# Packing the remainder rows and pacing the attention work of a four-layer transformer kernel

## The chip, the cores and the metric

The kernel runs on one core of one Trainium2 chip. The metric is the device time of one execution in microseconds (us). The engines are named as the profile names them: PE is TensorE (PEld its weight loads), DVE is VectorE, ACT is ScalarE, POOL is GpSimd. "L326" in a profile line is line 326 of the kernel's source. All runs quoted here were of the fast state. A ratio is the mean time of one kernel's fast runs over that of the other's of the same rounds, so not quite the ratio of the medians quoted beside it.

## The reference, cut to what matters

```
x = A_x                                               # 2048 tokens, 576 features
x = x + A(layernorm(x), A_wqkv, A_wo)
x = x + B(layernorm(x), B_w_gate, B_w_up, B_w_down)
x = x + A(layernorm(x), A_wqkv, A_wo)                 # the same weights again
x = x + B(layernorm(x), B_w_gate, B_w_up, B_w_down)

A: q, k, v = x @ wqkv, 32 heads of 18; a token attends to 8 tokens, itself and
   those 2, 4, .. 14 before it; softmax; @ wo
B: h = (x @ w_gate) * (x @ w_up)   # 576 -> 4608
   h @ w_down                      # 4608 -> 576
```

Both kernels work on chunks of 256 tokens. With 8 chunks and two layers of each kind there are 16 units of A (attention) and 16 stages of B (feed-forward). In B nearly all work is PE's. In A the products of q and k and the weighted sums of v are elementwise work on DVE, between short stretches of PE: transposes, projections, logits, broadcast of the weights, output. B of a chunk needs A of the same chunk and layer, and the second A of a chunk needs its first B.

## The kernel before

The parts that the argument touches. A bank is one of the buffers into which PE writes its sums (`psum` in the code); here ACT and DVE empty it before the next sum begins in it:

```
gu = [psum.tile([P, 2, CH], FP32, name=f"gu{i}") for i in range(2)]     # two gate/up banks
pa = [psum.tile([P, 512], FP32, name=f"pa{i}") for i in range(2)]       # two banks for A
...
def gate_up(ft):                      # one feature tile of 128, of 36
    ...
    ps = gu[ft % 2]
    for (hh, w_) in ((0, wg), (1, wu)):
        for k in range(KT):           # KT = 5: four full tiles and the remainder of 64 rows
            nc.tensor.matmul(ps[:, hh, :], lhsT=w_[:, k, ft * P:(ft + 1) * P], rhs=xnT[:, k, :], ...)
    ...
        nc.scalar.copy(g_sb[:], ps[:, 0, :])
        nc.vector.tensor_tensor(hT[:], ps[:, 1, :], g_sb[:], op=ALU.mult)
...
gate_up(0)
for ft in range(1, NFT):
    gate_up(ft)
    down(ft - 1)                      # down is one feature tile behind
...
for k in range(max(nA - 1, nB)):      # the whole of A comes ahead of B in the program
    ia = k + 1
    if ia < nA:
        a_head(ia)
        _drain(a_body(ia))
    if k < nB:
        for _ in b_body(k): ...       # b_head(k + 1) at two thirds of it
```

The order in which an engine takes its instructions is fixed when the program is compiled. The compiler's scheduling starts from the order of the program but moves instructions (the first experiment below shows it: six remainders of gate that were written ahead of six of up came out partly in pairs with them). That each engine then runs its own list in order on the chip is taken for granted here and was not tested.

Of the kernel before, what the change touches and what calls it, by code (L numbers as in the profile page):

```python
# [14 lines left out]
def _drain(gen):  # L15
    for _ in gen:
        pass


@with_exitstack  # L20
def kernel(
# [10 lines left out]
    nlayers: int = 4,  # L32
    mode: str = "seq",
# [8 lines left out]
    KT = (D + P - 1) // P  # L42
    DP = KT * P
    DHP = KT * 4
    CH = 256
    NCH = S // CH
    NST = CH // P
    SQ = CH // 4
    NFT = F // P
    G = 4  # L50
    while NFT % G:
        G -= 1
    qscale = float(Dh) ** -0.5
    assert D == 576 and S % CH == 0 and F % P == 0
# [4 lines left out]
    xbp = ctx.enter_context(tc.tile_pool(name="xbp", bufs=4))  # L59
    psum = ctx.enter_context(tc.tile_pool(name="psum", bufs=1, space=PSUM))  # L60
    st_pool = ctx.enter_context(tc.tile_pool(name="static", bufs=1))
    small = ctx.enter_context(tc.tile_pool(name="small", bufs=6))

    xv = A_x.rearrange("b (n p) d -> (b n) p d", p=P)
    ov = out.rearrange("b (n p) d -> (b n) p d", p=P)

    NXS = 3
    xf = [[xpool.tile([P, D], FP32, name=f"xf{s}_{i}") for i in range(NST)] for s in range(NXS)]

    def load_x(c):  # L70
        for i in range(NST):
            xb = xbp.tile([P, D], BF16, name="xb")
            nc.sync.dma_start(xb[:], xv[c * NST + i])
            nc.scalar.copy(xf[c % NXS][i][:], xb[:])  # L74

    nc.scalar.preload_act_table_set("natural_log_exp_and_others")
    load_x(0)

# [3 lines left out]
                            base=0, pattern=[[-1, P]], channel_multiplier=1)  # L82
    eps_t = consts.tile([P, 1], FP32, name="eps_t")
    nc.vector.memset(eps_t[:], 1e-5)
    xn_bufs = [st_pool.tile([P, DP], BF16, name=f"xnb{i}") for i in range(2)]
    for t_ in xn_bufs:
        nc.gpsimd.memset(t_[:, D:DP], 0.0)

    wqkv = wpool.tile([P, KT, 3, DHP, 32], BF16, name="wqkv")
    wo_p = wpool.tile([P, KT, D], BF16, name="wo_p")  # L90
    wg = wpool.tile([P, KT, F], BF16, name="wg")
    wu = wpool.tile([P, KT, F], BF16, name="wu")
    ksz = [min(P, D - k * P) for k in range(KT)]
    TL = D - (KT - 1) * P

    def load_rows(dst, src):
        for k in range(KT):
            nc.sync.dma_start(dst[:ksz[k], k, :], src[k * P:k * P + ksz[k], :])
        nc.sync.dma_start(dst[TL:2 * TL, KT - 1, :], src[(KT - 1) * P:D, :])

    startup_pool = tc.tile_pool(name="startup", bufs=1)
    sp = startup_pool.__enter__()
    wraw = sp.tile([P, KT, 3 * D], BF16, name="wraw")
    load_rows(wraw, A_wqkv)
    if NCH > 1:
        load_x(1)
    wo_v = A_wo.rearrange("(h d) n -> d h n", d=Dh)
    for d in range(DHP):
        t, g = d // 4, d % 4
        dd = d if d < Dh else d - 2  # L110
        nc.sync.dma_start(wo_p[32 * g:32 * g + 32, t, :], wo_v[dd])
    if nlayers > 1:
        load_rows(wg, B_w_gate)
        load_rows(wu, B_w_up)
    wd_v = B_w_down.rearrange("(g t p) d -> g p t d", p=P, t=G)

    accm = [psum.tile([P, 512], FP32, name=f"accm{i}") for i in range(NST)]
    acct = psum.tile([P, NST, 64], FP32, name="acct")
    gu = [psum.tile([P, 2, CH], FP32, name=f"gu{i}") for i in range(2)]
    pa = [psum.tile([P, 512], FP32, name=f"pa{i}") for i in range(2)]  # L120
    tps = psum.tile([P, KT, P], BF16, name="tps")

    NXT = 4
    xnT_bufs = [st_pool.tile([P, KT, CH], BF16, name=f"xnT{i}") for i in range(NXT)]
    qT = st_pool.tile([P, KT, CH], BF16, name="qT")
    kT = st_pool.tile([P, KT, HALO + CH], BF16, name="kT")
    vT = st_pool.tile([P, KT, HALO + CH], BF16, name="vT")
    Lt = st_pool.tile([P, W, SQ], FP32, name="Lt")
    a_c = st_pool.tile([P, W, SQ], BF16, name="a_c")
    ab = st_pool.tile([P, W, 4, SQ], BF16, name="ab")  # L130
    oT = st_pool.tile([P, KT, CH], BF16, name="oT")

    Erep = consts.tile([P, 4, 32], BF16, name="Erep")
    Erep2 = Erep[:].rearrange("p a b -> p (a b)")
    Bsel = consts.tile([P, 4, 4, 32], BF16, name="Bsel")
    n_alayers = (nlayers + 1) // 2
    halo_k = [consts.tile([P, KT, HALO], BF16, name=f"halo_k{l}") for l in range(n_alayers)]
    halo_v = [consts.tile([P, KT, HALO], BF16, name=f"halo_v{l}") for l in range(n_alayers)]
    wqf = wqkv[:].rearrange("p k t d h -> p k t (d h)")
    rot_box = {}  # L140

    def finish_startup():
        nc.gpsimd.memset(wqkv[:, :, :, Dh:DHP, :], 0.0)
        for t_ in halo_k + halo_v:
            nc.gpsimd.memset(t_[:], 0.0)
        for k in range(KT):
            src = wraw[:, k, :].rearrange("p (t h d) -> p t d h", t=3, h=H)
            if k % 2 == 0:
                nc.vector.tensor_copy(wqkv[:, k, :, 0:Dh, :], src)
            else:  # L150
                nc.scalar.copy(wqkv[:, k, :, 0:Dh, :], src)
        startup_pool.__exit__(None, None, None)
        nc.gpsimd.memset(Erep[:], 0.0)
        for g0 in range(4):
            nc.gpsimd.affine_select(out=Erep[:], in_=Erep[:], compare_op=ALU.not_equal, fill=1.0,
                                    base=-32 * g0, pattern=[[0, 4], [-1, 32]], channel_multiplier=1)
        nc.gpsimd.memset(Bsel[:], 0.0)
        for j in range(4):
            nc.gpsimd.affine_select(out=Bsel[:, j], in_=Bsel[:, j], compare_op=ALU.not_equal, fill=1.0,
                                    base=-32 * j, pattern=[[0, 4], [-1, 32]], channel_multiplier=1)  # L160
        rot_box["rot"] = ctx.enter_context(tc.tile_pool(name="rot", bufs=2))

    state = {"xn": 0, "pa": 0}
    wlist = [w ^ 1 for w in range(W)]

    def head(c, xnT):
        for i in range(NST):
            x = xf[c % NXS][i]
            st = small.tile([P, 2, 6], FP32, name="st")
            xr = x[:].rearrange("p (a b) -> p a b", a=2)  # L170
            for a in range(2):
                nc.vector.bn_stats(out=st[:, a, :], in_=xr[:, a, :])  # L172
            mv = small.tile([P, 2], FP32, name="mv")
            nc.vector.bn_aggr(out=mv[:], in_=st[:])
            rstd = small.tile([P, 1], FP32, name="rstd")
            nc.scalar.activation(rstd[:], mv[:, 1:2], ACT.Ln, bias=eps_t[:])
            nc.scalar.activation(rstd[:], rstd[:], ACT.Exp, scale=-0.5)
            nmr = small.tile([P, 1], FP32, name="nmr")
            nc.vector.tensor_scalar(nmr[:], mv[:, 0:1], rstd[:], -1.0, op0=ALU.mult, op1=ALU.mult)  # L179
            xn = xn_bufs[state["xn"] % 2]  # L180
            state["xn"] += 1
            nc.scalar.activation(xn[:, 0:D], x[:], ACT.Identity, bias=nmr[:], scale=rstd[:])  # L182
            for k in range(KT):
                nc.tensor.transpose(tps[:, k, :], xn[:, k * P:(k + 1) * P], ident[:])  # L184
            nc.scalar.copy(xnT[:, :, i * P:(i + 1) * P], tps[:])  # L185
            yield

    def next_pa():
        b = state["pa"] % 2
        state["pa"] += 1  # L190
        return b

    def phase_A(c, la, xnT, last):
        xs = xf[c % NXS]
        nc.scalar.copy(kT[:, :, 0:HALO], halo_k[la][:])
        nc.scalar.copy(vT[:, :, 0:HALO], halo_v[la][:])
        for t3, dst in ((0, qT), (1, kT), (2, vT)):
            for t in range(KT):
                b = next_pa()
                for k in range(KT):  # L200
                    nc.tensor.matmul(pa[b][:, 0:CH], lhsT=wqf[:, k, t3, t * P:(t + 1) * P], rhs=xnT[:, k, :],  # L201
                                     start=(k == 0), stop=(k == KT - 1))
                if t3 == 0:
                    nc.scalar.mul(dst[:, t, :], pa[b][:, 0:CH], qscale)
                else:
                    nc.scalar.copy(dst[:, t, HALO:HALO + CH], pa[b][:, 0:CH])  # L206
                yield
        nc.scalar.copy(halo_k[la][:], kT[:, :, CH:CH + HALO])
        nc.scalar.copy(halo_v[la][:], vT[:, :, CH:CH + HALO])
        for p_ in range(W // 2):  # L210
            prod = rot_box["rot"].tile([P, 2, KT, CH], BF16, name="prod", bufs=2)
# [12 lines left out]
            for j in range(4):  # L224
                nc.scalar.copy(Lt[32 * j:32 * j + 32, 2 * p_:2 * p_ + 2, :], lgv[32 * j:32 * j + 32, :, SQ * j:SQ * (j + 1)])  # L225
# [149 lines left out]
    if nB:  # L375
        b_head(0)
# [41 lines left out]
```

## Time and profile before

| | before |
|---|---|
| median time | 1268.2 us (12 runs, 1266.9 to 1269.5) |
| profiled span | 1267.2 us |
| first gate matmul, end of the last matmul | 71.3, 1263.2 us |
| length of a B stage in the middle | 75.5 us |

A window of one middle stage of the kernel before. The columns are the stretch and its length, busy us and instructions of each engine, granted PE clock, DMA share and GB/s:

```profile
core 0: us, PE busy (x) PEld busy (x) DVE busy (x) ACT busy (x) POOL busy (x), PEclk, DMA share, GB/s
451.80:527.30 75.50, 73.34 (x619) 54.29 (x628) 46.10 (x100) 34.22 (x94) 0.00 (x0) 1.00 0.24 72
```

No engine but PE is near the length of the stage, and DMA is at a quarter. PE's 73.3 us are busy time of overlapping records. The matmuls of the stage (B's 56.9 us and one A unit of 13.5) take 70.4 us by their spacing, so about 5 us of the 75.5 are loss. Stages are counted here from the last down matmul of one stage to that of the next.

The profile's view of what PE waited for, kernel before (total us, times, longest):

```profile
PE tps L184 <- ACT xnb L182: 19.3, 4, 11.2
PE pa L253 <- DVE a_c L249: 15.2, 16, 6.7
PE pa L272 <- DVE oT L266: 12.3, 1, 12.3
PE pa L222 <- DVE s L220: 7.6, 15, 4.6
PE accm L312 <- DVE hT L305: 7.1, 24, 0.6
```

The large ones with few counts are the start-up. This view shows only waits that outlast the modelled end of the matmul before, so it understates. From here on I use start-to-start times: the time from one matmul's start to the next one's, less the spacing that the same form has when nothing waits (109.2 ns for 256 columns, 216 for 512, 28 for 64, 122.5 for 288, 56 for a transpose; 216 more where a 512-column record is missing), summed over gaps of more than 8 ns and put to the matmul that came late.

### The profile page before, as it was taken

The page shows a single profiled execution, that of the slowest core. Times are in us where ns is not written, and L with a number is a line of the kernel's source. Part 1 is how long each engine was busy: PE and PEld are TensorE (multiplying, and loading weights), DVE is VectorE, ACT ScalarE, POOL GpSimd, SP SyncE. Part 2 cuts the span into 40 slices and gives each one's busy share as a digit, 9 for nine tenths or more (in the row PEclk, how much of TensorE's full clock was granted, in tenths as well). Part 3 has the DMA queues.
Part 4 walks back from the last instruction along what each step waited for, and adds up shares of the span by engine and source line. Part 5 has one row for each costly group of instructions (what it writes and reads, how often), then busy time and mean ns, then how long its engine had stood idle before and what let it go on. Part 6 is the DMA issues. An engine that isn't in the chain of part 4 may idle for free.

```text
span 1267.2 us, 24030 instructions
## 1 busy us (share of the span) xinstructions
PE 1178.5 (93%) x9873; PEld 875.6 (69%) x10032; DVE 745.6 (59%) x1602; ACT 559.8 (44%) x1523; POOL 4.8 (0%) x23
## 2 busy tenths in 40 slices
PE   4289999999999999999999999999999999999998
PEld 2056777767676776767677677776767777676776
DVE  4657365674846558375674736658384654837532
ACT  6254353545345354453634335354544534445321
POOL 1000000000000000000000000000000000000000
PEclk9589999999999999999999999999999999999999
DMA  7902212222231312312222231222222232222331
GB/s 260 300 28 65 87 57 83 68 74 77 76 97 56 92 57 76 94 57 76 76 76 66 76 94 57 76 60 73 84 76 79 63 83 68 76 79 57 92 103 48
DMA packets 83918, 105.95 MB, mean 84 GB/s; under 512 B 3424, under 2 KB 81888, under 8 KB 82528
## 3 DMA queue, kind: packets, MB, share of 16 engines
q1 hardware_dynamic: 83808, 104.41, 27.8%
q8 instruction: 78, 1.28, 0.4%
q14 instruction: 32, 0.26, 0.1%
HBM read 102.04 MB, written 2.36 MB: 82 GB/s over the span
## 4 chain that ended last, share of the span: by engine, by line
PE 53%; DVE 34%; ACT 10%; issue 2%; DMA 0%; SPq 0%; ACTq 0%; DVEq 0%
PE gu L299 27%; PE accm L312 10%; PE pa L201 8%; DVE oT L266 7%; DVE pv L265 6%; DVE prod L216 5%; DVE hT L305 5%; ACT ab L255 3%; PE pa L272 3%; PE acct L314 3%; PE tps L184 2%; ACT Lt L225 2%; DVE prod L217 2%; DVE st L172 1%; ACT xnb L182 1%
## 5 line engine op out<-in xcount | busy, mean ns | idle before, releaser
L305 DVE TENSOR_TENSOR hT<-gu,g_sb 128x256 bf16<-128x256 f32 x576 | 242.2, 421 | 310.7 <-ACT g_sb L304 309.8
L299 PE MATMUL gu<-xnT,wg 128*128 128x256 bf16 x2880 | 423.4, 273 | 0.0
L299 PE MATMUL gu<-xnT,wu 128*128 128x256 bf16 x2880 | 419.1, 273 | 0.0
L304 ACT CAST g_sb<-gu 128x256 bf16<-128x256 f32 x576 | 213.2, 370 | 429.3 <-PE gu L299 420.0
L312 PE MATMUL accm<-wdt,hT 128*128 128x512 bf16 x1001 | 324.9, 381 | 9.3 <-DVE hT L305 7.1
L299 PEld LDWEIGHTS <-wg 128*128 128x128 bf16 x2880 | 245.1, 98 | 90.3 <-issue 0.2
L299 PEld LDWEIGHTS <-wu 128*128 128x128 bf16 x2880 | 280.6, 98 | 36.9 <-issue 1.2
L314 PE MATMUL acct<-wdt,hT 128*128 128x64 bf16 x1152 | 221.9, 193 | 11.2 <-DVE hT L305 3.6
L312 PEld LDWEIGHTS <-hT 128*128 128x128 bf16 x1152 | 112.2, 97 | 119.3 <-DVE hT L305 40.7
L216 DVE TENSOR_TENSOR prod<-qT,kT 128x2560 bf16<-128x2560 bf16 x64 | 93.3, 1486 | 102.8 <-ACT kT L206 102.8
L201 PE MATMUL pa<-xnT,wqkv 128*128 128x256 bf16 x1200 | 145.5, 274 | 1.9 <-ACT xnT L185 1.5
L201 PEld LDWEIGHTS <-wqkv 128*128 128x128 bf16 x1200 | 117.5, 98 | 29.5 <-issue 4.5
L314 PEld LDWEIGHTS <-hT 128*128 128x128 bf16 x1152 | 112.8, 98 | 9.9 <-issue 2.1
L266 DVE TENSOR_TENSOR oT<-oT,pv 128x1280 bf16<-128x1280 bf16 x112 | 91.6, 818 | 0.6
L265 DVE TENSOR_TENSOR pv<-vT,ab 128x1280 bf16<-128x1280 bf16 x112 | 89.9, 818 | 0.0
L225 ACT COPY Lt<-pa 32x128 f32<-32x128 f32 x256 | 65.6, 256 | 34.8 <-PE pa L222 31.6
L182 ACT ACTIVATE xnb<-xf,nmr,rstd 128x576 bf16<-128x576 f32 x64 | 55.5, 869 | 12.0 <-DVE nmr L179 11.6
L272 PE MATMUL pa<-wo_p,oT 128*128 128x288 bf16 x320 | 46.6, 295 | 14.0 <-DVE oT L266 12.3
L185 ACT COPY xnT<-tps 128x640 bf16<-128x640 bf16 x64 | 44.1, 689 | 21.7 <-PE tps L184 20.7
L172 DVE BATCH_NORM_STATS2 st<-xf 128x6 f32<-128x288 f32 x128 | 51.6, 439 | 2.8 <-ACT xf L74 2.8
L184 PE MATMUL tps<-ident,xnb 128*128 128x128 bf16 x320 | 30.0, 227 | 22.4 <-ACT xnb L182 19.3
L272 PEld LDWEIGHTS <-oT 128*128 128x128 bf16 x320 | 30.7, 100 | 28.9 <-DVE oT L266 19.1
(57 smaller groups left out, 538.7 us busy)
## 6 DMA issues: line engine op xcount, KB each, us to landing
wdt<-in_B_w_down_dram SPq DMA_DIRECT2D x144, 576.0 KB, 4.0
wg<-in_B_w_gate_dram SPq DMA_DIRECT2D x4, 1152.0 KB, 8.7
wu<-in_B_w_up_dram SPq DMA_DIRECT2D x4, 1152.0 KB, 21.9
xb<-in_A_x_dram SPq DMA_DIRECT2D x16, 144.0 KB, 3.5
out_dram<-ob SPq DMA_DIRECT2D x16, 144.0 KB, 4.0
wraw<-in_A_wqkv_dram SPq DMA_DIRECT2D x4, 432.0 KB, 5.3
wg<-in_B_w_gate_dram SPq DMA_DIRECT2D x2, 576.0 KB, 15.7
wu<-in_B_w_up_dram SPq DMA_DIRECT2D x2, 576.0 KB, 23.8
```

The costliest lines, as they stand in the source:

```text
L182: nc.scalar.activation(xn[:, 0:D], x[:], ACT.Identity, bias=nmr[:], scale=rstd[:])
L201: nc.tensor.matmul(pa[b][:, 0:CH], lhsT=wqf[:, k, t3, t * P:(t + 1) * P], rhs=xnT[:, k, :], start=(k == 0), stop=(k == KT - 1))
L216: nc.vector.tensor_tensor(prod[:], q2, k2, op=ALU.mult)
L225: nc.scalar.copy(Lt[32 * j:32 * j + 32, 2 * p_:2 * p_ + 2, :], lgv[32 * j:32 * j + 32, :, SQ * j:SQ * (j + 1)])
L265: nc.vector.tensor_tensor(pv[:], vT[:, :, o0:o0 + CH], abw, op=ALU.mult)
L266: nc.vector.tensor_tensor(oT[:], oT[:], pv[:], op=ALU.add)
L272: nc.tensor.matmul(pa[hh][:, 0:HD], lhsT=oT[:, t, i * P:(i + 1) * P], rhs=wo_p[:, t, hh * HD:(hh + 1) * HD], start=(t == 0), stop=(t == KT ...
L299: nc.tensor.matmul(ps[:, hh, :], lhsT=w_[:, k, ft * P:(ft + 1) * P], rhs=xnT[:, k, :], start=(k == 0), stop=(k == KT - 1), skip_group_chec ...
L304: nc.scalar.copy(g_sb[:], ps[:, 0, :])
L305: nc.vector.tensor_tensor(hT[:], ps[:, 1, :], g_sb[:], op=ALU.mult)
L312: nc.tensor.matmul(accm[i][:], lhsT=hT[:, i * P:(i + 1) * P], rhs=wdt[:, ft % G, 0:512], start=(ft == 0), stop=(ft == NFT - 1))
L314: nc.tensor.matmul(acct[:, i, :], lhsT=hT[:, i * P:(i + 1) * P], rhs=wdt[:, ft % G, 512:D], start=(ft == 0 and i == 0), stop=(ft == NFT - ...
```

## The change

The intent is to give PE less to do and to keep it from waiting. The diff, cut to its core (cuts marked by "..."):

```
-    gu = [psum.tile([P, 2, CH], FP32, name=f"gu{i}") for i in range(2)]
+    bk = [psB.tile([P, 512], FP32, name=f"bk{i}") for i in range(6)]
...
+        nc.sync.dma_start(wg[0:TL, KF, fs], B_w_gate[KF * P:D, fs])     # TL = 64, KF = 4
+        nc.sync.dma_start(wg[TL:P, KF, fs], B_w_up[KF * P:D, fs])
...
+        def remainders(g):
+            for pair in range(3):
+                for e in range(2):
+                    ft = g * GF + 2 * pair + e
+                    fresh = pair == 2 and e == 0
+                    mm(bk[2 * pair], e, wg, ft, KF, 0, TL, fresh)
+                    mm(bk[2 * pair + 1], e, wg, ft, KF, TL, P, fresh)
...
+        for part in range(NFT // NH):                                   # two halves of 18 tiles
+            for g in range(part * NH // GF, (part + 1) * NH // GF):     # groups of 6 tiles
+                for b in range(4):
+                    fulls(g, b, True)
+                    yield 0.87 * NT / 2
+                remainders(g)
+                evac(0)
+                evac(1)
+                fulls(g, 4, False)
+                yield 1.8 * NT / 2
+                fulls(g, 5, False)
+                evac(2)
+                yield 0.87 * NT / 2
...             # then down for all 18 tiles, then x is added to
...
+    DL_LN, DL_PR, DL_LG, DL_SM, DL_AV = 10.0, 3.0, 12.0, 9.0, 2.5
...
+            else:                       # in the A unit, behind the products, ahead of the logits
+                yield 0.0, (DL_PR if p_ < 3 else DL_LG) * NT / 2
...
+    seq = [(pairs[0], 0), (pairs[1], 0)]
+    for c in range(2, len(pairs)):
+        seq += [(pairs[c], 0), (pairs[c - 2], 1)]
...
+        while nexta[0] < n and nexta[0] <= upto and len(active) < 2:
...
+            finish_A(k)
+            for dur in B_gen(k, tiles, lb == 1):
+                clock[0] += dur
+                pump(k + 2, 2)
```

In words: gate's and up's remainder of 64 rows share one weight tile and run as two row tiles (matmuls over half of PE's rows each, which can stand in PE side by side), into different banks. Going from full matmuls to row tiles or back is called a mode change below. B has six banks, which are emptied 512 wide. Down runs after 18 tiles and not one tile behind. Projections take 14 column tiles and not 15, and logits use four 32-column tiles. An A unit is a generator whose steps are put between B's steps by a clock in the program: a step says how long its successor should be held back. Two units may be active, up to two stages ahead. Normalisation moves from ACT to DVE, products are cut from 2560 to 1280 elements.

## The prediction

> **What bounds the kernel now.** I read the page first: busy times, the 40 slices, the groups of instructions.
>
> ```profile
> span 1267.2 us, 24030 instructions
> PE 1178.5 (93%) x9873; PEld 875.6 (69%) x10032; DVE 745.6 (59%) x1602; ACT 559.8 (44%) x1523; POOL 4.8 (0%) x23
> ...
> PE   4289999999999999999999999999999999999998
> ...
> DMA  7902212222231312312222231222222232222331
> ```
>
> TensorE (PE) is at 9 tenths or more from the fourth slice to the last but one; the first three slices, about 95 us, are a start-up in which it is mostly idle. The DMA engines are loaded only there. But busy PE says little, since pipelined matmuls overlap in the records. So I read the timeline of PE in the last feed-forward (B) stage, where no attention (A) work is left, for start-to-start times:
>
> ```profile
> 1238.18 0.71 PE L299 MATMUL gu<-xnT,wg 128*128 128x256 bf16 x5
> 1238.72 0.71 PE L299 MATMUL gu<-xnT,wu 128*128 128x256 bf16 x5
> 1239.27 0.38 PE L312 MATMUL accm<-wdt,hT 128*128 128x512 bf16 x1
> 1239.48 0.19 PE L314 MATMUL acct<-wdt,hT 128*128 128x64 bf16 x1
> 1239.51 0.38 PE L312 MATMUL accm<-wdt,hT 128*128 128x512 bf16 x1
> 1239.73 0.19 PE L314 MATMUL acct<-wdt,hT 128*128 128x64 bf16 x1
> 1239.76 0.71 PE L299 MATMUL gu<-xnT,wg 128*128 128x256 bf16 x5
> ```
>
> One feature tile of 128 takes 1239.76 - 1238.18 = 1.58 us: ten 256-column matmuls at 109 ns (five in 0.54), and two pairs of 512 and 64 columns at 216 + 28 ns. Nothing waits there. The same reading gives 122 ns for 288 columns and 56 ns for a transpose, weight load included.
>
> Work of the kernel before at these rates: gate/up 5760 x 0.109 = 628 us; down 1152 x 0.244 = 281 (the page has 1001 of the 1152 accm records, but all 1152 of their weight loads). An A unit: 75 projections x 0.109 = 8.2, logits 4 x 0.216 = 0.9, broadcast the same, output 20 x 0.122 = 2.4, transposes 20 x 0.056 = 1.1: 13.5 us. Fifteen A units run inside the B stages: 202. Sum 1111 us.
>
> The timeline of the start gives where this begins, and the waits of PE where the rest is:
>
> ```profile
> 18.17 11.33 PE L201 MATMUL pa<-xnT,wqkv 128*128 128x256 bf16 x75 [1.31 <-ACT xnT L185]
> ...
> 59.87 2.58 PE L272 MATMUL pa<-wo_p,oT 128*128 128x288 bf16 x10 [12.33 <-DVE oT L266]
> ...
> 71.29 1.27 PE L299 MATMUL gu<-xnT,wg 128*128 128x256 bf16 x5
> ```
>
> The first A unit runs alone until 71.3. The last matmul ends at 1263.2. So 1192 us hold 1111 us of matmuls: about 81 us, 5 us a stage, are PE standing still or waiting in its queue, which the busy share hides. Two groups point at the cause:
>
> ```profile
> L305 DVE TENSOR_TENSOR hT<-gu,g_sb 128x256 bf16<-128x256 f32 x576 | 242.2, 421 | 310.7 <-ACT g_sb L304 309.8
> ...
> L216 DVE TENSOR_TENSOR prod<-qT,kT 128x2560 bf16<-128x2560 bf16 x64 | 93.3, 1486 | 102.8 <-ACT kT L206 102.8
> ```
>
> With two gate/up banks, a bank must be emptied within about one 1.58 us tile, and a 1.49 us `prod` on VectorE (DVE) can stand ahead of the emptying. Gaps before a down matmul that needs hT, by start-to-start times, come to roughly 27 us; gaps before the A matmuls (transposes, logits, broadcast, output), in order behind DVE or ACT, to nearly 40; projections waiting for one of two banks to 8.
>
> **What the Trainium skill says.** "TensorE: Matmul & The Clock Gate", the part on 56 against 53.3 ns, gives a warm spacing of N / 2.4 GHz + 2.5 ns: 109 ns at 256 columns, 216 at 512. The trace agrees. "TensorEngine Tiling (Array Packing)", Key Properties, says that tiles can load and multiply in parallel but that changing the tiling mode drains TensorE; its Restrictions add that different row tiles may not use one PSUM bank at once. No run here shows either yet; the change puts gate and up in different banks. "TensorE: Matmul & The Clock Gate", Part 3, measured 3.07 times for four row tiles, so packing works, though not perfectly. "VectorE: DVE Perf Modes", the tier table, has tensor_tensor at 2x for bf16 in SBUF and 1x from PSUM: 1280 bf16 elements took 818 ns here and 512 from PSUM 687, which agrees.
>
> **The change, part by part.**
>
> 1. Gate and up contract over 576 = 4 x 128 + 64 rows. Before, the 64 remaining rows cost a full matmul each for gate and up. Now gate's remainder lies in rows 0-63 and up's in rows 64-127 of one weight tile, as two row tiles that can run at once. Full matmuls: 576 x 8 x 0.109 = 503 us. Remainder pairs: 576 x 0.112 = 65 if they overlap; the weight loads fit, since a transpose shows load plus multiply at 56 ns. Twelve remainders stand together per six tiles, so 96 groups enter and leave the mode: 192 switches. A matmul lasts 273 ns but is spaced 109, so at most about 164 ns of drain per switch; I take 120, an estimate: 23 us. Total 591 against 628: 37 saved.
> 2. Projections pack q, k and v into 14 column tiles, not 15: 5 x 0.109 = 0.55 us a unit. Logits use four 32-column tiles side by side, 0.25 us and not 0.86. An A unit falls from 13.5 to 12.3 us; fifteen save 18. The second unit's normalisation and projections (8 us) are admitted into the start-up's holes.
> 3. Evacuations become 512 wide and B gets six banks. DVE empties 288 pairs at about 0.69 us, 198 against 242; ACT 288 at 0.59, 169 against 213. Six tiles take about 6 us of PE, and after the remainders the next group asks for bank 0 in 1.7 us, bank 1 in 2.6 and bank 3 in 4.4, while copy and multiply need about 1.5 per pair. So a full DVE operation may stand in the way, and none is longer than 0.82 us, since `prod` is cut from 2560 to 1280. I expect most of the 27 us to vanish, and the 8 with it.
> 4. Down runs in two halves of 18 tiles. Its matmuls are unchanged; DVE adds to x twice, 64 x (0.69 + 0.22) = 58 us against 29, beside the matmuls.
> 5. DVE elsewhere: `prod` and its sums 8 x (0.82 + 0.42 + 2 x 0.28) = 14.4 against 12.0 us a unit, 38 more; normalising moves from ACT to DVE, 64 x about 0.55 = 35 more. DVE sums to 745 - 44 + 29 + 38 + 35, less 13 for nmr, with a little else about 800 to 870 us: 70 to 80% of the new span, no bound on average. ACT loses 55 (xnb), 56 (64-row logit copies merged), 44 and 11 (x cast).
> 6. Start-up: x goes to the statistics without a cast, permuting q no longer waits for k and v, and v's projections move behind the products. Projections can start near 14 rather than 18, products at 23 rather than 27; products are 1 us slower, the final normalisation is batched. First B matmul near 67, against 71.
> 7. Two A units are active at once, released by a clock in the program that holds back a matmul until its DVE work should be done. This aims at the 40 us of A gaps.
>
> **The sum.** Start-up 67. Matmuls after it: 503 + 65 + 23 + 281 + 15 x 12.3 - 8 = 1048. Residual waits 28 (81 before, less the evacuation part, less half of the A part). Last additions and store 4, as before. Total 1147 us.
>
> **Rivals.** (a) The two row tiles do not overlap: each remainder costs 109 and part 1 becomes 503 + 126 + 23 = 652, worse than before; the time would be near 1208. For it: nothing in the profile of before shows packed rows. Against: the skill's measurement. (b) DVE becomes the bound in a stage. A stage would hold about 54 us of DVE by record against 66 of PE; pipelined DVE records overlap by some 80 ns each, so the real load is less. If A matmuls queue behind DVE as they did, waits stay at 80 and the time is 1200. (c) Start-up lengthens because two A units share DVE: products of the first queue behind statistics of the second, 5 to 10 us, so 1155. (d) Switches are free and the pacing works fully: 1048 - 23 + 67 + 4 + 10, about 1106.
>
> **Range and chances.** The work terms are firm to about 20 us, apart from overlap; the waits may be 10 to 70. I predict 1147 us, with 1110 to 1195 to hold 8 times in 10. Faster by over 2% means under 1243: all rivals lie below that, and only two of them together, or a scheduling accident, would pass it. Faster 0.94, within 2% 0.04, slower 0.02.
>
> **What would show it.** The remainder matmuls as starts of gate and up a few ns apart and pairs about 112 ns apart (right), or 218 (rival a). The gap from the last full matmul to the first remainder and back: 120 ns beyond spacing. The first full gate matmul near 67 us. PE waits on hT near zero, DVE in a middle stage under 55 us, and the stage length near 67 rather than 74.5. The prediction is wrong if start-to-start sums of matmuls after the start-up are not near 1050, or if the waits beyond them are not near 28.

## The result and the profile after

The changed kernel takes 1142.6 us (8 runs, 1141.7 to 1143.3) against 1268.2 us, ratio 0.9009 (0.9000 to 0.9017). The prediction was 1147 us, with a range of 1110 to 1195.

The page of the changed kernel: span, busy times, slices of PE and DVE (40 equal parts of the span, busy tenths of each), and the chain that ended last.

```profile
span 1141.4 us, 23604 instructions
...
PE 1081.0 (95%) x9886; PEld 807.2 (71%) x9952; DVE 785.1 (69%) x1707; ACT 374.4 (33%) x761; POOL 8.4 (1%) x28
...
PE   4379999999999999999999999999999999999998
...
DVE  4796768587687775678766776877768587666222
...
PE 78%; DVE 19%; ACT 1%; issue 1%; DMA 0%; DVEq 0%; SPq 0%; ACTq 0%
```

DVE's share rose from 59 to 69%, though the span is a tenth shorter, and PE is still the engine that is full. In the chain the share of PE rose to 78% (it was 53%, with 34% for DVE): DVE now stands beside PE's work more often and between its pieces less often.

A middle stage of the changed kernel, and its second stage (same columns as the window before):

```profile
624.20:691.50 67.30, 66.88 (x620) 50.07 (x623) 51.40 (x116) 23.29 (x49) 0.00 (x0) 1.00 0.29 89
143.00:218.80 75.80, 71.46 (x634) 52.35 (x639) 55.08 (x130) 25.29 (x54) 0.00 (x0) 0.95 0.23 71
```

The stage fell from 75.5 to 67.3 us with DVE at 51.4. The second stage is 8 us longer than a middle one. Its mean granted clock is 0.95, since the trace has two stretches of 3.4 us at half clock in it, from 145.4 and from 196.6 us; just ahead of the second, PE stood 2.19 us before an output matmul.

Groups of instructions (busy us and mean ns; idle before and releaser), to be set beside the down line of before, given first, and the hT line of before in the prediction:

```profile
L312 PE MATMUL accm<-wdt,hT 128*128 128x512 bf16 x1001 | 324.9, 381 | 9.3 <-DVE hT L305 7.1
...
L326 PE MATMUL bk<-xnTb,wg 128*128 128x256 bf16 (+1 forms) x3456 | 374.8, 273 | 0.2 <-ACT xnTb L178 0.2
L381 PE MATMUL bk<-wdt,hT 128*128 128x512 bf16 x1086 | 289.6, 380 | 1.1 <-ACT g_sb L350 1.0
L351 DVE TENSOR_TENSOR hT<-bk,g_sb 128x512 bf16<-128x512 f32 x288 | 189.5, 685 | 129.2 <-ACT g_sb L350 96.4
```

The second line, the first of the changed kernel, holds 2304 full gate matmuls and, as a second form, all 1152 remainders, since both halves lie in wg. Hardly any idle time stands before these matmuls of B. The timeline of PE in a late stage shows a group being entered:

```profile
1057.35 1.04 PE L326 MATMUL bk<-xnTb,wg 128*128 128x256 bf16 x8
1058.22 1.04 PE L326 MATMUL bk<-xnTb,wu 128*128 128x256 bf16 x8
1059.19 1.26 PE L326 MATMUL bk<-xnTb,wg 64*128 64x256 bf16 x15
```

Eight full matmuls take 0.87 us, start to start; the eight ahead of the remainders take 0.97. The last line merges the twelve remainders with the first three full matmuls behind them. Inside, taken from the single records, the starts of a typical group follow each other so:

```
12 remainders, ns from one start to the next: 4 116 4 106 3 106 3 106 3 106 3 | 202 to the next full matmul
```

The two halves start 3 to 4 ns apart and a pair takes 109 to 120. Entering the mode costs 205 - 109 = 96 ns, leaving it 202 - 109 = 93.

Where the 125.8 us of span went, by start-to-start times:

| part of the span | before | after | predicted after |
|---|---|---|---|
| until the first gate matmul | 71.3 | 72.8 | 67 |
| gate/up at its spacing, with mode changes | 629.0 | 503.2 + 83.3 | 503 + 65 + 23 |
| down at its spacing | 281.1 | 281.1 | 281 |
| A's matmuls after the first gate matmul | 202.0 | 174.5 | 177 |
| what is left before the last matmul's end: waits, small costs | 79.8 | 22.9 | 28 |
| last additions and store | 4.1 | 3.6 | 4 |

83.3 us are 54.0 between starts of remainders, 19.8 behind the last one of a group, and 9.5 of extra time ahead of the first. Of A's 27.5 us, 14.3 are projections (131 fewer after the first gate matmul at 0.109: five fewer in each of 15 units, 56 moved into the start-up) and 13 are logits (60 x 0.216). The narrow logits are not free, though: the four of a unit start 3 to 4 ns apart, but in a typical unit the first comes 202 ns after a gate matmul (93 more than its spacing) and the next matmul 322 ns after the last (106 more than the 216 of its width). That is about 0.43 us a unit, against 0.86 before and 0.25 in the prediction. For all units it is 6.8 us, which stand in the last-but-one row, and 16.1 of that row's 22.9 us are waits. So the largest gain, 63 us (79.3 to 16.1), is waiting that went away; gate/up gave 42, and A 21 and not 27.

### The profile page after: what moved, and what is told of

Its sections match the earlier page's. It is cut to its first block, busy times and chain, and to the rows that moved or that the text cites. A ratio compares the mean times of both kernels' runs of the same rounds, so it can differ in the third digit from the quotient of the medians.

```text
span 1141.4 us, 23604 instructions
## 1 busy us (share of the span) xinstructions
PE 1081.0 (95%) x9886; PEld 807.2 (71%) x9952; DVE 785.1 (69%) x1707; ACT 374.4 (33%) x761; POOL 8.4 (1%) x28
## 4 chain that ended last, share of the span: by engine, by line
PE 78%; DVE 19%; ACT 1%; issue 1%; DMA 0%; DVEq 0%; SPq 0%; ACTq 0%
PE bk L326 46%; PE bk L381 15%; PE qkv L209 9%; DVE prod L235 5%; PE bk L383 3%; PE po L305 3%; DVE prod L236 2%; DVE s L237 1%; PE tps L177 1%; DVE st L155 1%; DVE s L238 1%; DVE pv L294 1%; DVE oT L295 1%; DVE hT L351 1%; PE pb L281 1%
## 5 line engine op out<-in xcount | busy, mean ns | idle before, releaser
L326 PE MATMUL bk<-xnTb,wg 128*128 128x256 bf16 (+1 forms) x3456 | 374.8, 273 | 0.2 <-ACT xnTb L178 0.2
L326 PEld LDWEIGHTS <-wg 128*128 128x128 bf16 (+1 forms) x3456 | 264.0, 97 | 73.0 <-issue 41.9
L326 PE MATMUL bk<-xnTb,wu 128*128 128x256 bf16 x2304 | 299.8, 273 | 1.5 <-DVE hT L351 1.5
L381 PE MATMUL bk<-wdt,hT 128*128 128x512 bf16 x1086 | 289.6, 380 | 1.1 <-ACT g_sb L350 1.0
L351 DVE TENSOR_TENSOR hT<-bk,g_sb 128x512 bf16<-128x512 f32 x288 | 189.5, 685 | 129.2 <-ACT g_sb L350 96.4
L350 ACT CAST g_sb<-bk 128x512 bf16<-128x512 f32 x288 | 159.1, 587 | 301.2 <-PE bk L326 269.4
L383 PE MATMUL bk<-wdt,hT 128*128 128x64 bf16 x1152 | 222.0, 193 | 3.6 <-issue 0.2
L209 PE MATMUL qkv<-xnTa,wq 128*128 128x256 bf16 x1120 | 138.4, 277 | 0.1
L209 PEld LDWEIGHTS <-wq 128*128 128x128 bf16 x1120 | 110.0, 99 | 17.7 <-issue 0.8
L235 DVE TENSOR_TENSOR prod<-qT,kT 128x1280 bf16<-128x1280 bf16 x128 | 102.8, 816 | 20.2 <-ACT kT L225 20.2
L177 PE MATMUL tps<-ident,xn 128*128 128x128 bf16 x320 | 30.1, 227 | 21.5 <-DVE xn L166 18.8
L283 ACT CAST ab<-pb 128x512 bf16<-128x512 f32 x64 | 37.2, 585 | 25.3 <-PE pb L281 25.2
```

The costliest lines, as they stand in the source:

```text
L177: nc.tensor.transpose(tps[:, k, :], xn[:, k * P:(k + 1) * P], ident[:])
L209: nc.tensor.matmul(ps[:, m, :], lhsT=wq[:, kk, c_:c_ + P], rhs=xnT[:, kk, :], start=(m == 0 and kk == 0), stop=(kk == KT - 1), skip_group_ ...
L235: nc.vector.tensor_tensor(prod[:], qT[:, :, 0:ch], kT[:, :, o0:o0 + ch], op=ALU.mult)
L326: nc.tensor.matmul(bank[:, e * ch:(e + 1) * ch], lhsT=w_[lo:hi, k_, ft * P:(ft + 1) * P], rhs=xnT[lo:hi, k_, :], start=start, stop=(not st ...
L350: nc.scalar.copy(g_sb[:].rearrange("p e s -> p (e s)"), bk[2 * pair][:, 0:2 * ch])
L351: nc.vector.tensor_tensor(hT[:].rearrange("p e s -> p (e s)"), bk[2 * pair + 1][:, 0:2 * ch], g_sb[:].rearrange("p e s -> p (e s)"), op=AL ...
```

## The experiments

All are correct against the reference. Times are medians; the changed kernel has 1142.6 us, the kernel before 1267.7 to 1268.3 in the rounds of these runs.

The waits of PE after the first gate matmul, in us, by the matmul that came late. Known costs of mode changes are taken off, so the sums are a little under the last-but-one row above. "Gate/up" includes waits at the start of a stage:

| kernel | down for hT | logits | broadcast | output | transposes | projections | gate/up | sum |
|---|---|---|---|---|---|---|---|---|
| before | 28.7 | 8.3 | 14.2 | 5.4 | 9.3 | 11.9 | 1.5 | 79.3 |
| before, down two tiles behind | 1.9 | 10.3 | 20.6 | 13.4 | 10.3 | 11.5 | 7.4 | 75.3 |
| before, A put in line later | 30.6 | 2.8 | 3.6 | 0 | 16.3 | 11.9 | 1.5 | 66.8 |
| changed | 1.4 | 0.1 | 0 | 5.6 | 2.5 | 0 | 5.9 | 16.1 |
| changed, no pacing | 13.9 | 21.5 | 9.1 | 23.6 | 19.4 | 5.6 | 12.4 | 105.7 |
| changed, one unit at a time | 0 | 0 | 0 | 121.8 | 57.3 | 0 | 50.9 | 230.0 |

(The changed kernel has 0.5 more ahead of remainders, the one without pacing 0.3.)

Not all of these times are PE standing still. The traces have stretches in which the granted clock is one half (with one unit at a time, 6.8 us of it behind each long pause), and matmuls that start about twice their spacing apart there are counted too. They are about 64 us of the 230.0 with one unit at a time, 14 of the 105.7 without pacing, and at most 2.5 in each of the other four rows.

### The remainders: order

```
-            for pair in range(3):
-                for e in range(2):
+            for half, lo, hi in ((0, 0, TL), (1, TL, P)):
+                for pair in range(3):
+                    for e in range(2):
...
-                    mm(bk[2 * pair], e, wg, ft, KF, 0, TL, fresh)
-                    mm(bk[2 * pair + 1], e, wg, ft, KF, TL, P, fresh)
+                        mm(bk[2 * pair + half], e, wg, ft, KF, lo, hi, fresh)
```

> The changed kernel with the twelve remainders of a group in another order: first the six of gate (rows 0 to 63), then the six of up (rows 64 to 127), so that neighbours use the same rows. Same matmuls, same number of mode changes. If the gain of the packed remainders comes from two row tiles running at once, ten of twelve starts now stand 109 ns apart and not every second one: a group costs 12 x 109 = 1.31 us instead of 6 x 112 = 0.67, 96 groups cost 61 us more, and the time is near 1200 us. Rival: a matmul of 64 rows is cheap by itself, or PE has slack there; then the time stays within 10 us of 1143.

Measured: 1162.6 us, 20 more and neither of the two. The trace says why (a typical group):

```
12 remainders, ns from one start to the next: 119 109 9 101 18 91 18 91 18 109 110 | 202
```

The compiler's scheduling did not keep the order. The short gaps show four pairs still running side by side; two pairs were lost, and the two lone halves on each side stand 109 ns apart. Two lost pairs x 109 ns x 96 groups are 21 us, which fits the 20, but the run is not the test that it was meant to be. A change of program order has to be looked up in the compiled order before it is trusted.

### The remainders: the first part undone alone

```
-    NWD = 8
+    NWD = 7
+    zs2 = ...                # two tiles of zeros for each half, filled below
...
             transposes(xns[i], xnT, i)
+            for h, lo, hi in ((0, 0, TL), (1, TL, P)):
+                nc.scalar.copy(zs2[h][k % 2][lo:hi, i * P:(i + 1) * P], xnT[lo:hi, KF, i * P:(i + 1) * P])
...
-                    mm(bk[2 * pair], e, wg, ft, KF, 0, TL, fresh)
-                    mm(bk[2 * pair + 1], e, wg, ft, KF, TL, P, fresh)
+                    for h in range(2):
+                        nc.tensor.matmul(bk[2 * pair + h][:, e * ch:(e + 1) * ch], lhsT=wg[:, KF, ft * P:(ft + 1) * P],
+                                         rhs=zs2[h][k % 2][:, 0:ch], start=fresh, stop=False, skip_group_check=True)
```

> The changed kernel with the first part undone alone: the remainders are multiplied with all 128 rows, each against its own right-hand tile in which the other's 64 rows are zero, so no mode changes and nothing runs side by side (seven and not eight weight buffers, and four short ACT copies more a unit, to make room and to fill these tiles). 1152 matmuls x 0.109 = 126 us against the 83 us that pairs and mode changes take in the changed kernel: 43 us more, near 1186. The first experiment's order was paired again by the compiler's scheduling, so this is the clean test. Rival: the packed rows gave less than it seems, as PE would have waited there anyway: 1143 to 1165.

Measured: 1182.0 us (ratio to before 0.9327, 0.9314 to 0.9340), 39.4 more than the changed kernel. The waits stayed low (11.3 us by the count of the table), so the difference is PE's work. Packing the remainders is worth 39 us here; the prediction said 37.

### The remainders: the cost of a mode change

```
                 for b in range(4):
                     fulls(g, b, True)
+                    if b == 1:
+                        remainders(g, (0,))
                     yield 0.87 * NT / 2
-                remainders(g)
+                remainders(g, (1, 2))
```

> The changed kernel with the remainders of the first pair of banks taken right after that pair's full matmuls, so that each group of six tiles enters and leaves the 64-row mode twice and not once. In the changed kernel the last full matmul before a remainder is followed after 205 ns and the last remainder after 202, 96 and 93 ns over the usual 109. If that is a drain paid at each change, 96 more visits cost 96 x 0.19 = 18 us: near 1161. Rival: the drain is paid only because other waits fall there; then within 5 us of 1143.

Measured: 1158.7 us, 16.1 more. The trace has 194 groups of remainders instead of 97 (a few were split by a matmul of A that the compiler put inside); nearly all are still entered at 205 ns behind a 256-column matmul and left at 201 or 202. The expectation of 18 holds to 2 us: the cost is paid at each change, about 0.17 us for a visit (in and out) by the total and 0.19 by the starts; the total is the smaller as PE waited some 4 us less elsewhere. Grouping twelve remainders was worth doing.

### The pacing

```
-    DL_LN, DL_PR, DL_LG, DL_SM, DL_AV = 10.0, 3.0, 12.0, 9.0, 2.5
+    DL_LN, DL_PR, DL_LG, DL_SM, DL_AV = 0.0, 0.0, 0.0, 0.0, 0.0
```

> The changed kernel with the five delays of the program's clock set to zero: an attention unit's next matmuls are put in line as soon as the unit is next in turn. If the pacing is what took away the waits of PE before attention matmuls (nearly 40 us before, about 10 after), they come back: 1165 to 1185. Rival: the order that the compiler's scheduling makes, and the late down matmuls, took them away, and the pacing adds little: within 10 us of 1143.

Measured: 1238.2 us, 95.6 more. Both expectations were too small. Without these five constants three quarters of the whole gain are lost. What PE waited for in this kernel, by the profile's view of the waits:

```profile
PE tps L177 <- DVE xn L166: 31.3, 18, 10.0
PE lg L250 <- DVE s L238: 31.2, 12, 10.4
PE po L305 <- DVE oT L295: 30.0, 15, 10.6
PE pb L281 <- DVE a_c L276: 9.8, 9, 5.7
```

and the same view of the changed kernel:

```profile
PE tps L177 <- DVE xn L166: 18.8, 5, 10.2
PE po L305 <- DVE oT L295: 16.0, 3, 12.6
PE lg L250 <- DVE s L238: 10.4, 1, 10.4
```

In the changed kernel these few are the start-up's. Without delays they recur in most stages: 18, 12 and 15 times. By the table the waits are 105.7 us against 16.1, and the first gate matmul comes at 78.3 us and not 72.8; the two make up 95 of the 99 us by which the two profiled runs differ.

### One unit at a time

```
-        while nexta[0] < n and nexta[0] <= upto and len(active) < 2:
+        while nexta[0] < n and nexta[0] <= upto and len(active) < 1:
```

> The changed kernel with at most one attention unit active at a time. If two units at once are needed to hide the attention chain (59 us long alone in the start-up, against stages of about 67 us in which DVE also serves the feed-forward), PE waits at the ends of stages: 1160 to 1250, though the start-up shortens by some 5 us as its DVE is not shared. Rival: one unit at a time is enough, and the shorter start-up shows: 1135 to 1143.

Measured: 1356.9 us, 214 more, far outside the 1160 to 1250 expected, and slower than the kernel before (ratio 1.0704). A middle stage of this kernel:

```profile
624.00:706.00 82.00, 71.81 (x621) 52.31 (x622) 48.61 (x107) 22.60 (x47) 0.00 (x0) 0.92 0.22 66
```

Every stage but the first and last takes 82 us, though DVE is busy for only 48.6 of them. PE near the start of that stage:

```profile
630.32 4.50 PE L305 MATMUL po<-wo,oT 128*128 128x288 bf16 x20 [6.07 <-DVE oT L295]
...
640.17 1.86 PE L326 MATMUL bk<-xnTb,wg 128*128 128x256 bf16 x8 [0.84 <-ACT xnTb L178]
641.83 1.91 PE L326 MATMUL bk<-xnTb,wu 128*128 128x256 bf16 x8
```

PE stands before output, transposes and the next gate matmul, and then runs slowly: the eight gate matmuls take 1.66 us from start to start where eight usually take 0.87, and the granted clock from 640.0 to 644.4 us is 0.50. Of the 121.8, 57.3 and 50.9 us of the table about 94, 53 and 19 are standing, the rest this slower running. With the delays, the chain of a unit takes longer than the 67 us of a stage in the changed kernel (PE waits for it at every stage here), so these delays need two units in flight. Whether one unit without delays would do is not shown: it was not run. The start-up was shorter, with the first gate matmul at 66.6 us, as expected.

### The kernel before with a third gate/up bank

```
-    gu = [psum.tile([P, 2, CH], FP32, name=f"gu{i}") for i in range(2)]
-    pa = [psum.tile([P, 512], FP32, name=f"pa{i}") for i in range(2)]
-    tps = psum.tile([P, KT, P], BF16, name="tps")
+    gu = [psum.tile([P, 2, CH], FP32, name=f"gu{i}") for i in range(3)]
+    psA = ctx.enter_context(tc.tile_pool(name="psA", bufs=2, space=PSUM))   # for pa and tps
...
-            ps = gu[ft % 2]
+            ps = gu[ft % 3]
```

> The kernel before with a third PSUM bank for gate/up (the transposes share the two banks of the attention matmuls); down still one feature tile behind. The prediction put the waits on hT (about 27 us) to a bank that must be emptied within a tile. If that is the cause, a third bank takes most of it away: 1268 less some 20, near 1248. Rival: it is the down matmul, which stands one tile (1.09 us of gate/up) behind its hT, that waits; a further bank changes nothing there: within 8 us of 1268.

Measured: 1263.1 us, ratio 0.9966 (0.9953 to 0.9978): 4.3 us by the ratio, under the rival's bound of 8. Waits before down were still 23.7 us, and the sum was 74.9.

### The kernel before with short products

```
-            nc.vector.tensor_tensor(prod[:], q2, k2, op=ALU.mult)
-            nc.vector.tensor_tensor(prod[:, :, 0:4:2, :], prod[:, :, 0:4:2, :], prod[:, :, 1:4:2, :], op=ALU.add)
+            for h_ in range(2):
+                nc.vector.tensor_tensor(prod[:, h_:h_ + 1], q2[:, h_:h_ + 1], k2[:, h_:h_ + 1], op=ALU.mult)
+                nc.vector.tensor_tensor(prod[:, h_, 0:4:2, :], prod[:, h_, 0:4:2, :], prod[:, h_, 1:4:2, :], op=ALU.add)
```

> The kernel before with each 2560-wide product and its first sum cut in two, so that no DVE operation is over 0.82 us; 128 more DVE instructions. If long DVE operations ahead of the emptying are what makes PE wait, most of the 27 us goes: near 1250. Rival: the wait comes from the chain of copy and multiply itself beside other DVE and ACT work, whatever the length; then within 8 us of 1268.

Measured: 1265.6 us, ratio 0.9982 (0.9975 to 0.9988): 2.3 us. Waits before down fell from 28.7 to 19.5, those before the logits rose from 8.3 to 17.7, and the sum was 79.0 against 79.3. What was gained at one place was paid back at another.

### The kernel before with down two tiles behind

```
-            hT = rot_box["rot"].tile([P, CH], BF16, name="hT", bufs=3)
+            hT = rot_box["rot"].tile([P, CH], BF16, name="hT", bufs=4)
...
-            down(ft - 1)
+            if ft > 1:
+                down(ft - 2)
             yield
+        down(NFT - 2)
         down(NFT - 1)
```

> The kernel before with down two feature tiles behind gate/up and not one (four hT buffers, gate/up still two banks). If the wait is that of a down matmul for hT one tile behind, its room grows from 1.09 to about 2.7 us and the 27 us of gaps go: near 1245. Rival, the prediction's own words: the bank must be emptied within a tile; two banks stay two, and nothing is gained: within 8 us of 1268.

Measured: 1262.6 us, ratio 0.9960 (0.9946 to 0.9973): 5.1 us. The first half of the expectation is right and the second is wrong. The waits before down are gone, 28.7 to 1.9 us, with two banks as before, so it was down's place and not the banks. But the sum fell only from 79.3 to 75.3. The profile's view of this kernel's waits shows where they went, the broadcast at 21.2 us (it was 15.2) and the output 16 times instead of once:

```profile
PE pa L272 <- DVE oT L266: 22.0, 16, 12.3
PE pa L253 <- DVE a_c L249: 21.2, 16, 6.7
```

Between the projections and the output of a unit, DVE's and ACT's chain sets the pace, and the compiled order puts a nearly fixed amount of B's matmuls between the points where PE needs that chain: in the traces 30 or 34 gate/up matmuls stand between a unit's last logits and its first broadcast before, 31 or 36 here, and 86 or 87 between broadcast and output in both. Take away a wait in B and PE is only earlier at the next A matmul.

### The kernel before with the attention work later in line

```
-            _drain(a_body(ia))
-        if k < nB:
-            n = 0
-            for _ in b_body(k):
-                n += 1
-                if n == (NFT * 2) // 3 and k + 1 < nB:
+            a = a_body(ia)
+            for _ in range(16):
+                next(a)
+        PACE = {6: 1, 8: 1, 11: 1, 13: 1, 18: 9, 31: 1, 32: 9}
+        if k < nB:
+            n = 0
+            for _ in b_body(k):
+                n += 1
+                for _ in range(PACE.get(n, 0)):
+                    if ia < nA:
+                        next(a, None)
+                if n == 32 and k + 1 < nB:
...          # and a step of the unit ends ahead of each logits matmul, not behind it
```

> The kernel before with its attention work put in line later: the logits, broadcast and output matmuls of a unit are emitted at set feature tiles of the running feed-forward stage, one to two tiles after DVE should be done with their inputs (broadcast 5, output 8 tiles later than before), and the next stage's normalisation at tile 32 and not 24. Banks, lag and DVE work as they were. Three changes that took away waits on hT or shortened DVE operations left the stage at 75.5 us, since the attention matmuls then waited longer. If it is the early place of the attention matmuls that costs PE some 5 us a stage, a stage falls to about 72 and the time to 1200 to 1230. Rival: the wait follows the chain wherever it is put; then it shows at the stage's end, and the time is 1255 or more.

Measured: 1255.7 us, ratio 0.9902 (0.9889 to 0.9916): 12.4 us, at the rival's edge and well short of the 38 to 68 expected. By the table, logits, broadcast and output fell together from 27.9 to 6.4 us, which is what the later place was to do (50 gate/up matmuls now stand between logits and broadcast, 124 between broadcast and output). The waits before down stayed (30.6), and those before transposes rose by 7, as the normalisation ahead of the next stage had only four tiles left. In the order of the kernel before, a unit must begin and end inside one stage, so it cannot be held back much further. The two single repairs together, late down and later A, were not run; that they would add up is open.

### The width of the emptying

```
-                nc.scalar.copy(g_sb[:].rearrange("p e s -> p (e s)"), bk[2 * pair][:, 0:2 * ch])
-                nc.vector.tensor_tensor(hT[:].rearrange("p e s -> p (e s)"), bk[2 * pair + 1][:, 0:2 * ch],
-                                        g_sb[:].rearrange("p e s -> p (e s)"), op=ALU.mult)
+                for e in range(2):
+                    nc.scalar.copy(g_sb[:, e, :], bk[2 * pair][:, e * ch:(e + 1) * ch])
+                    nc.vector.tensor_tensor(hT[:, e, :], bk[2 * pair + 1][:, e * ch:(e + 1) * ch],
+                                            g_sb[:, e, :], op=ALU.mult)
```

> The changed kernel with each 512-wide copy and multiply that empties a pair of gate/up banks cut in two of 256, as wide as before the change. DVE gets 288 x (2 x 0.42 - 0.69) = about 44 us more, ACT the same. If the width of the emptying matters for the time (the prediction's third part), waits of PE come back in part: 1150 to 1165. Rival: DVE and ACT are off the path and six banks with late down matmuls hide it: within 5 us of 1143.

Measured: 1138.3 us, 4.3 less than the changed kernel and so on the rival's side (ratio to before 0.8977, 0.8965 to 0.8990, against 0.9009). DVE's busy time rose from 785.1 to 801.2 us, by 16 and not by 44, and PE waited less: 11.8 us and not 16.1, the second stage 73.0 us and not 75.8. So the 512-wide emptying is no part of the gain here. Why the narrow one is a little better (shorter operations ahead of others, or only another compiled order) is not settled.

### The start-up: the second unit late

```
     def finish_A(k):
...
-            admit(k + 1)
+            admit(k + (k > 0))
```

> The changed kernel with the second attention unit admitted only when the first feed-forward stage begins, not in the start-up. If sharing DVE, ACT and PE with it is what made the start-up 72.8 us and not 67, the first gate matmul comes at 65 to 68. Whether that helps the whole: the 13 us of its matmuls move into the first stages, and the second stage must wait for it, so I expect the total no better, 1143 to 1155. Rival: the start-up stays near 72, as it was the first unit's own chain that was misjudged.

Measured: 1155.4 us, 12.7 more, with the first gate matmul at 67.0 us. The first number is as expected, the second just above its range. The first gate matmul of this kernel:

```profile
67.02 1.86 PE L326 MATMUL bk<-xnTb,wg 128*128 128x256 bf16 x8 [0.84 <-ACT xnTb L178]
```

The second stage then takes 87.6 us, as it waits for its unit: 5.8 us saved at the start, and the first two stages together 18 us longer.

### The start-up: the second unit behind the first one's products

```
-            admit(k + 1)
+            admit(k + (k > 0 or any(a[3] >= 3 for a in active)))
```

> The changed kernel with the second attention unit admitted in the start-up only after the first one's products are in line, between admitting it at once (first gate matmul at 72.8 us) and only in the first stage (67.0 us, but 12.7 us slower in all). If what delays the first unit is the second one's normalisation and transposes ahead of its projections, the first gate matmul comes near 69 and the total near 1139. Rival: the products of the second unit and its projections ahead of the broadcast delay it, and these stay; then no change, within 2 us of 1143.

Measured: 1138.0 us, ratio to before 0.8975 (0.8963 to 0.8988), 4.7 less than the changed kernel. PE at the start of the changed kernel:

```profile
12.36 0.29 PE L177 MATMUL tps<-ident,xn 128*128 128x128 bf16 x1 [1.56 <-DVE xn L168]
17.44 1.25 PE L177 MATMUL tps<-ident,xn 128*128 128x128 bf16 x10 [4.79 <-DVE xn L166]
...
19.53 9.56 PE L209 MATMUL qkv<-xnTa,wq 128*128 128x256 bf16 x70
...
72.78 1.51 PE L326 MATMUL bk<-xnTb,wg 128*128 128x256 bf16 x8
```

and of this kernel:

```profile
12.59 1.04 PE L177 MATMUL tps<-ident,xn 128*128 128x128 bf16 x6 [1.56 <-DVE xn L168]
15.82 9.41 PE L209 MATMUL qkv<-xnTa,wq 128*128 128x256 bf16 x70 [2.19 <-ACT xnTa L178]
...
68.03 1.87 PE L326 MATMUL bk<-xnTb,wg 128*128 128x256 bf16 x8
```

In the changed kernel PE waits from 12.7 us for a DVE normalisation that ends at 17.4, the second unit's. The first unit's own last normalisation had ended at 12.85 us, so its transposes stood in PE's list behind the second unit's. In this one the first unit's transposes go through at once and the first projections start 3.7 us earlier. The first gate matmul comes at 68.0 us. The later stages are as before, so nearly all of the 4.8 us at the start stay in the total. This kernel and the one with narrow emptying are the two fastest, and their intervals overlap; a kernel with both was not run.

## Why the prediction was right

The predicted total was 1147 us and the measured one 1142.6. The errors partly offset each other: the start-up was put 6 us too short and the waits, taken without the narrow logits, 12 us too long. That is in part luck; the work was right to about 1 us.

**The matmul work** was predicted at 1048 us after the start-up, and 503.2 + 83.3 + 281.1 + 174.5 = 1042.1 were measured, 1048.9 with the 6.8 us of narrow logits, which the prediction counts as work (at 3.8 us, without their mode changes). The terms of the remainders were 65 for pairs and 23 for 192 switches at an estimated 120 ns; measured are 64 (480 steps between pairs at about 112 ns and 96 last ones at 109) and 18 (96 + 93 ns a visit), and the full-row experiment gives 39 for the saving of 37. Rival (a), row tiles that do not overlap, is out: the halves start 3 to 4 ns apart.

**The start-up** was predicted at 67 us and came at 72.8. The estimate for the first unit by itself was right, 67.0 with the second unit kept out; the step that failed is the claim that the second unit goes "into the start-up's holes", free of charge. Rival (c) had the size right, 5 to 10 us against 5.8, but looked for it in DVE's queue. For 4.8 of the 5.8 us the traces show another place, PE's list: the second unit's transposes, not ready until 17.4 us, stood ahead of the first unit's, ready at 12.85. Admitting the second unit somewhat later removes this part.

**The waits** were predicted at 28 us and the row shows 22.9 (16.1 without known costs). So the waits proper were overestimated by 12 us, and of the reasons only some were right. Waits before down and before projections nearly vanished, as predicted (28.7 to 1.4 and 11.9 to 0), but those of A's other matmuls fell from 37.2 to 8.2 us and not by half, and gate/up rose from 1.5 to 5.9. That the figure for down came true is luck as far as the mechanism goes. The prediction put the 27 us before down to a bank that "must be emptied within about one 1.58 us tile" behind a long product, and expected six banks, 512-wide emptying and short products to take them away. A third bank gave 4 us, short products 2, and narrow emptying cost nothing. In the kernel before, what takes these waits away is that down no longer stands one tile behind its hT; in the changed kernel this was not undone alone (nor were the six banks), and without the delays 13.9 us of waits before down are there although down is late. And taking them away alone pays 5 us, since PE then waits at A's matmuls. The term "half of the A part" for the pacing was far too small for what the pacing does: without the delays 90 us come back by the table (14 of the 105.7 as slower running), in B's places and in A's. Rival (d), full pacing with free switches, was nearer on pacing and wrong on switches.

**DVE** was predicted at 800 to 870 us of busy time and has 785; a middle stage was to have under 55 us and has 51.4, and the stage near 67 us has 67.3. Rival (b), DVE as the bound of a stage, is out: even the second stage has only 55.1 us of it in 75.8. One reading of the page was off, without effect on the sum: of the three slices called mostly idle the third is busy for 8 tenths, and the start-up ends at 71.3 and not at 95 us.

## What to carry to other kernels

Where one engine runs a compiled list in order and waits at many places for a chain on other engines, removing one kind of wait mostly moves it to the next place; sum all waits of that engine over a stage before and after, not the one that was aimed at. Waits go when the dependent work is put later in the list than the chain needs. With one unit of the chain in flight that took the waits from 79.3 to 66.8 us here, with two, in the changed kernel, to 16.1 with all else that was changed; taking away the delays cost 95.6 us and taking away the second unit 214, more than any other part that was undone. These losses overlap and do not add up. A contraction remainder of half the rows is worth packing as two row tiles if enough of them stand together to pay the mode change, about 0.19 us in and out here; a pair saves about 0.11 us (two spacings of 109 ns less 112), so by this estimate two pairs pay a visit.

## What the Trainium skill lacked or had wrong

- "TensorEngine Tiling (Array Packing)", Key Properties, says that changing the tiling mode drains TensorE and gives no figure. These runs show one: from full matmuls to 64-row tiles 96 ns and back 93 ns beyond the 109 ns of a 256-column matmul. Doubling the visits cost 16 us for 97 more. The 32-column tiles of the logits show 93 ns in and 106 out.
- "TensorE: Matmul & The Clock Gate", Back-to-back issue gap, gives a sustained roofline in streams of load and multiply of about 81 ns at 128 columns and 131 ns at 512. Here each matmul has its own weight load, and the spacing is 56 ns for 128-column transposes and 216 ns for 512 columns: what that section calls the isolated gap.
- No page that I read says that a wait removed on an engine with a fixed order comes back at its next wait: 26.8 us less before down, 4 us less in the sum (the kernel before with down two tiles behind).
